# The first batch's queries, scores and masks put earlier, and a first mixer group that begins over two of three blocks of channels

## The chip, the cores and the metric

One core of a Trainium2 chip runs the whole kernel. The metric is device time in microseconds (us), the median over several executions. The kernel before takes 480.65 us (480.13 to 480.83 in 3 executions). Engines are called PE (TensorE), PEld (its weight loads), ACT (ScalarE), DVE (VectorE), POOL (GpSimd) and SP (SyncE, which issues the DMAs). "L223" is line 223 of the kernel before.

## The reference

Two stages, over 4 batches of 768 positions and 8 heads of 48 channels (384 in all):

```python
# attention, per batch and head
f = 1 / (1 + exp(-f_logit))
for t in range(S):
    state = f[t][:, None] * state + outer(k[t], v[t])
    y[t] = q[t] @ state
# x: y with the heads side by side, (batch, 768, 384)
# mixer
h = (x.transpose(0, 2, 1) @ U @ V).transpose(0, 2, 1)   # U 768 x 32, V 32 x 768
u = x + h
out = u + relu(u @ w_ch1) @ w_ch2                       # 384 x 1536, 1536 x 384
```

The mixer's weights come as 8-byte floats and are turned into 4-byte ones on the chip.

## The kernel before, in words

**Attention.** A unit is one pair of heads of one batch, so there are 16, four in a batch (`HP` = 4). A unit's 768 positions are cut into 12 chunks of 64. For each chunk the kernel forms scores of queries against keys (`scores`, L843), masks them (`mask`, L856 on DVE), multiplies them with v (`inner`, L948), makes the chunk's contribution to the state (`states`, L891, copied to `added` by ACT in L898), and joins the contributions to running states with a scan on DVE (`scan`, L913), which are then read with the queries (`read`, L930). `kept` (L870, copy L874) turns the weighted keys. The front half of a unit prepares its operands: `gates` (transposes L680, sigmoid on ACT, L742 and L743 in later batches), `keep` (scan of the gates' logs L747 on DVE, then the copy L752 on ACT), `keys`, `read_back`, and `queries` (transposes L680, then DVE L692). `front(n, ...)` and `rear(n, ...)` hand out these pieces of unit n by name. The results are copied into `x` (L954).

**Mixer.** The low rank part is L223 (`low_rank_of`), L232 (`added_up_of`) and L248 (`mix_of`), ending in additions to `x` on DVE (L197). Then pairs of position blocks (groups `a` = 0, 1, 2) are turned by `turn(a)` (six transposes L261 and one ACT copy L262) and multiplied: `ch1(a, j)` is 12 products L273 of 128 x 256 and one relu L283 on ACT, over columns 2j and 2j + 1 of w_ch1 in pieces of 128; `ch2` is L298. `ps_mm`, the pool of PSUM banks for most of these, has two buffers.

**Weights.** U, two parts of V, 12 column slices of w1 and 12 row slices of w2 are brought in by `weight_loader`. Each has four parts: `start` (a DMA of 8-byte words, L82), `halves` (ACT L91, L92), `join` (DVE L98, L99, L100) and, at the end of `join`, POOL's L101, which writes the slice. A conversion of a slice means all of halves and join. `ahead_by(n, weights)` makes a list of calls, each of which starts the transfer n places further on and converts its own slice. The first six slices of w1 are loaded into spare z buffers (`held` makes them free), all later ones into four buffers `w_raw`.

**Order.** Inside `manual_schedule` the order on PE, DVE and ACT is that of the code, written by hand; SP's loads are in the code's order as well up to `written.close()`. The first batch's four units run one after another with their pieces interleaved by hand; its mixer's first part follows, and then a loop in which the mixer's `ch1` pieces of the first batch, one conversion of a slice each, and (from piece `EARLY` on) pieces of the second batch's units alternate. What is left of the conversions is done after the loop. Two small fillers, `warm(2)` and `warm(3)` (L217), are products whose results nobody reads, each of 128 x 128 in a bank already in use; `busy` is the same on a bank of its own.

Of the kernel before, what the change touches and what calls it, by code (L numbers as in the profile page):

```python
# [10 lines left out]
F32 = mybir.dt.float32  # L11
# [100 lines left out]
def ahead_by(n, loads):  # L112


    def call(i):
        if i + n < len(loads):
            loads[i + n][0]()
        loads[i][1]()

    return [lambda i=i: call(i) for i in range(len(loads))]  # L120
# [36 lines left out]
class Mixer:  # L157
# [6 lines left out]
    def __init__(self, tc, b, x, U, V, w1, w2, sums, ident, blocks, out, two, three, zp, ps_big, ps_mm, wide=False,  # L164
                 z_all=None, room=None, pair=0):
        nc = tc.nc
        P = nc.NUM_PARTITIONS
        NCH, DM = x.shape[1], x.shape[2]
        R, FF = U.shape[2], w1.shape[2]
        NG = P // R  # L170
        NDC, NFC = DM // P, FF // P
# [39 lines left out]

        hs, last = {}, {}

        def warm(n):

            for _ in range(n):
                nc.tensor.matmul(last["pm"][:, DM : DM + P], lhsT=ident, rhs=ident, start=True, stop=True)  # L217

        def low_rank_of(cols):
            pm = last["pm"] = ps_mm.tile([P, 512], F32, name="ph", tag="mm")  # L220
            for c in range(NCH):
                g = slice((c % NG) * R, (c % NG + 1) * R)
                nc.tensor.matmul(pm[g, cols], lhsT=U[:, c, :], rhs=x[:, c, cols],  # L223
                                 start=(c < NG), stop=(c >= NCH - NG))
            if not hs:
                for i in range(2):
                    hs[i] = two.tile([P, DM], F32, name="h", bufs=2)
            nc.scalar.copy(hs[0][:, cols], pm[:, cols])

        def added_up_of(cols):  # L230
            pm = last["pm"] = ps_mm.tile([P, 512], F32, name="ph", tag="mm")
            nc.tensor.matmul(pm[:, cols], lhsT=blocks, rhs=hs[0][:, cols], start=True, stop=True)  # L232
            nc.scalar.copy(hs[1][:, cols], pm[:, cols])

# [15 lines left out]
                xv = bass.AP(a.tensor, a.offset, [list(a.ap[0]), [DM, 2], [NG * DM, m], [1, n]])  # L250
                add(xv, xv, pm, ALU.add)

        self.some = low_rank_of, added_up_of, mix_of, warm

        def turn(a):

# [10 lines left out]
        def ch1(a, j):  # L267

            pm = ps_mm.tile([P, 512], F32, name="pz", tag="mm")
            for i in range(2):  # L270
                for m in range(NDC):
                    o = (2 * j + i) * P
                    nc.tensor.matmul(pm[:, i * 2 * P : (i + 1) * 2 * P], lhsT=w1[:, m, o : o + P],  # L273
                                     rhs=uT[a][:, m, :], start=(m == 0), stop=(m == NDC - 1))
            c, k = divmod(2 * j, NI)
            if k == 0:

                if z_all is not None and not (wide and c == 1):
                    i = a if wide else (2 * a + c) % 3
                    z[a, c] = z_all[:, i * NI : (i + 1) * NI, :]  # L280
                else:
                    z[a, c] = zp.tile([P, NI, 2 * P], F32, name="zw" if wide and c == 1 else "z")
            nc.scalar.activation(z[a, c][:, k : k + 2, :].rearrange("p i t -> p (i t)"), pm, AF.Relu)  # L283

        def store(t, o):
            nc.sync.dma_start(out=out[b, t * P : (t + 1) * P, :], in_=o)
# [201 lines left out]
def factored_path(ctx, tc, q, k, v, f_logit, moe_U, moe_V, moe_w_ch1, moe_w_ch2, out, ok):  # L488
# [475 lines left out]
    def front(n, *names):  # L964

        if n >= NU:
            return []
        if n not in ahead:
            ahead[n] = dict(zip(("gates", "keep", "keys", "read_back", "queries"), prepare(n)))
        return [ahead[n].pop(nm) for nm in names]  # L970

    def rear(n, *names):

        if not 0 <= n < NU:
            return []
        if n not in here:
            here[n] = dict(zip(("kept", "states", "scan", "scores", "read", "inner", "mask", "spread"), attend(n)))
        return [here[n].pop(nm) for nm in names if nm in here[n]]
# [53 lines left out]
    with tc.manual_schedule(engines={nc.vector.engine, nc.scalar.engine}):  # L1032


        idle = ps_mm.tile([P, 512], F32, name="idle", tag="mm")

        def busy(n, cols=DM):
            for _ in range(n):
                nc.tensor.matmul(idle[:, 0:cols], lhsT=blank[:, 0:P], rhs=blank[:, 0:cols], start=True, stop=True)

        written = ExitStack()
        written.enter_context(tc.manual_schedule(engines={nc.sync.engine}))
        busy(3)
        for piece in front(0, "gates", "read_back", "keep"):
            piece()
        load(1, "k", "q")
        load(2, "f")
        load(1, "v")
        loads = ahead_by(early + FIRST, weights)
        halves, join = [[w[i] for w in weights[:early]] for i in (2, 3)]  # L1050
        done, rest = slice(0, 2 * (HP - 1) * D), slice(2 * (HP - 1) * D, DM)

        def held():
            for i in range(2, FIRST, 2):
                t = zp.tile([P, NFC // 2, 2 * P], F32, name="zw").rearrange("p i t -> p (i t)")
                nc.scalar.copy(t[:, 0:1], x_tiles[0][:, 0, 0:1])
                spare.extend([t.bitcast(U64)[:, 0:WP], t.bitcast(U64)[:, WP : 2 * WP]])
            for load_w in weights[early + 2 : early + FIRST]:
                load_w[0]()
            load(HP, "f", "k", "q", "v")  # L1060

        for n in range(HP):
            last = n + 1 == HP
            pieces = rear(n - 1, "scan", "mask") + front(n, "keys")
            if last:
                pieces += join[:1]
            if n == 0:
                pieces += front(n, "queries") + rear(n, "spread", "kept") + [lambda: busy(1, 2 * P)]
                pieces += front(n + 1, "gates") + rear(n, "scores", "states") + front(n + 1, "read_back", "keep")
                for piece in pieces:  # L1070
                    piece()
                load(2, "k", "q")
                load(3, "f")
                load(2, "v")
                continue
            pieces += rear(n, "spread") + rear(n - 1, "read") + rear(n, "kept")
            if last:
                pieces += halves[1:2] + front(n, "queries") + rear(n - 1, "inner") + [held] + join[1:2] + rear(n, "states")
                pieces += halves[2:] + rear(n, "scores")
            else:  # L1080
                pieces += rear(n - 1, "inner") + front(n + 1, "gates") + front(n, "queries") + rear(n, "states", "scores")
                pieces += (halves[:1] if n + 2 == HP else []) + front(n + 1, "read_back", "keep")
            for piece in pieces:
                piece()
            if n == 1:
                weights[0][0]()
                load(3, "k", "q")
                for load_w in weights[1:early]:
                    load_w[0]()
                load(3, "v")  # L1090
                for load_w in weights[early : early + 2]:
                    load_w[0]()
        m = mixer(0)
        low_rank_of, added_up_of, mix_of, warm = m.some
        for piece in rear(n, "scan", "mask") + join[2:]:
            piece()
        for load_w in weights[early + FIRST : early + FIRST + early]:
            load_w[0]()
        load(HP + 1, "f", "k", "q", "v")
        written.close()  # L1100
        low_rank_of(done)
        warm(2)
        loads[early]()
        for piece in rear(n, "read"):
            piece()
        added_up_of(done)
        for piece in rear(n, "inner"):
            piece()
        mix_of(done, range(0, NBL - 2, 2))
        low_rank_of(rest)  # L1110
        mix_of(done, range(NBL - 2, NBL, 2))
        added_up_of(rest)
        mix_of(rest)
        warm(3)
        loads[early + 1]()
        for t in [starts] + fz:
            nc.vector.memset(t, 0.0)
        loads = loads[early + 2 :]

        start = m.before[3:5] + m.firsts[0:1] + m.before[5:]  # L1120

        EARLY = 6
        second = chain(front(HP, "gates", "keep", "keys", "read_back", "queries"), steps(HP, 2 * HP + 1))
        for i, (_, piece) in enumerate(start + m.firsts[1:]):
            piece()
            if loads:
                loads.pop(0)()
            if i >= EARLY:
                next(second)()
        for f in loads:  # L1130
            f()
        n = len(m.seconds) // (NBL // 2)
        todo, after = m.seconds[:-n], m.seconds[-n:]

        attention(second, 12 + 10 * HP - (len(start) + len(m.firsts) - 1 - EARLY), todo)
        m = start_mixer(1, after)
        for f in to_sum:
            f()
# [380 lines left out]
```

## Time and profile before

| | before |
|---|---|
| median of 3 executions | 480.65 us |
| profiled execution | 480.69 us |
| its span | 479.0 us |
| mean granted TensorE clock | 0.999 |
| PE busy | 462.1 us (96%) |
| PEld busy | 399.0 us (83%) |
| DVE busy | 346.0 us (72%) |
| ACT busy | 181.0 us (38%) |
| POOL busy | 36.1 us (8%) |

The span is the time between the first and the last record of the core; 1.7 us of the execution lie around it. Busy shares are averages over the whole span. A row of the timeline gives the start and the duration in us, the engine, the line, the operation and its tiles, and in brackets the idle time of that engine before it with the work that ended it. PE rows of many products are drawn together ("x48").

### The profile page before, as it was taken

Reading aid. Unit: us, or ns where it says so; the run is one execution under the profiler, and the core shown is the slowest. Engines: PE = TensorE matmul, PEld = TensorE weight load, DVE = VectorE, ACT = ScalarE, POOL = GpSimd, SP = SyncE. Lnnn points to the kernel's source line nnn. Section 1 sums busy time; section 2 is a strip of 40 time slices with the busy share of each in tenths; the row PEclk is TensorE's granted clock in tenths of the full one; section 3 lists DMA queues with packets and bytes.
Section 4 is the critical chain, followed back from the end, with each engine's and each line's share of the span. In section 5 each row is a group of like instructions: output and inputs, shape, how many; then the busy total and the mean of one; then the engine's idle time right before and its main releaser. Section 6 shows DMA issues by size and latency. Waiting matters only on the chain.

```text
span 479.0 us, 12800 instructions
## 1 busy us (share of the span) xinstructions
PE 462.1 (96%) x5557; PEld 399.0 (83%) x5557; DVE 346.0 (72%) x557; ACT 181.0 (38%) x338; POOL 36.1 (8%) x48
## 2 busy tenths in 40 slices
PE   7989999999999899999999999999999999999995
PEld 5876888876665478798899888899979999999995
DVE  4557978798999575767766547997796886858642
ACT  5675766664444123434341423542311311212200
POOL 2001445442000000000000000000000000000000
PEclk9999999999999999999999999999999999999999
DMA  9988996667787422253425200100000000000001
GB/s 145 151 160 219 210 235 156 161 117 103 115 120 117 84 41 26 26 77 78 64 38 100 41 33 3 27 3 21 16 1 1 35 1 18 18 0 34 1 34 40
DMA packets 158680, 34.36 MB, mean 72 GB/s; under 512 B 149206, under 2 KB 157078, under 8 KB 158614
## 3 DMA queue, kind: packets, MB, share of 16 engines
q1 hardware_dynamic: 158614, 33.44, 38.2%
q8 instruction: 46, 0.75, 0.7%
q14 instruction: 20, 0.16, 0.1%
HBM read 28.70 MB, written 4.72 MB: 70 GB/s over the span
## 4 chain that ended last, share of the span: by engine, by line
PE 75%; DVE 11%; ACT 5%; issue 3%; DMA 3%; SPq 1%; POOL 0%; DVEq 0%; ACTq 0%
PE pw L327 26%; PE pz L273 20%; PE pp L425 12%; PE sc L843 2%; PE y L948 2%; PE y L930 2%; DVE late L765 2%; PE po L298 2%; DVE late L747 1%; DVE added L913 1%; PE put L261 1%; PE pt L870 1%; PE ds L891 1%; PE pt L710 1%; PE pu L207 1%
## 5 line engine op out<-in xcount | busy, mean ns | idle before, releaser
L273 PE MATMUL pz<-uT,w 128*128 128x256 f32 x504 | 114.7, 382 | 1.8 <-ACT z_all L283 1.3
L273 PEld LDWEIGHTS pz<-uT,w 128*128 128x128 f32 x504 | 93.7, 190 | 15.8 <-ACT z_all L283 2.1
L327 PE MATMUL pw<-w,z_all 128*128 128x192 f32 x216 | 37.7, 329 | 0.0
L327 PE MATMUL pw<-zw,w_raw 128*128 128x192 f32 x216 | 37.3, 327 | 0.0
L327 PEld LDWEIGHTS pw<-zw,w_raw 128*128 128x128 f32 x216 | 35.2, 190 | 0.7 <-DVE w_raw L197 0.6
L327 PEld LDWEIGHTS pw<-w,z_all 128*128 128x128 f32 x216 | 35.0, 190 | 0.7
L101 POOL TENSOR_TENSOR w<-w_y,w_r 128x384 int32<-128x384 int32 x24 | 31.5, 1313 | 40.0 <-DVE w_y L100 34.4
L283 ACT ACTIVATE z_all<-pz 128x512 f32<-128x512 f32 x33 | 19.7, 597 | 33.0 <-PE pz L273 32.9
L425 PE MATMUL pp<-v_nat,late 128*128 128x128 f32 x224 | 28.8, 275 | 0.0
L425 PEld LDWEIGHTS pp<-v_nat,late 128*128 128x128 f32 x224 | 27.0, 192 | 0.0
L418 ACT ACTIVATE other<-other 128x512 f32<-128x512 f32 x18 | 11.3, 633 | 39.9 <-DVE other L197 39.9
L918 ACT COPY st<-added 128x576 f32<-128x576 f32 x12 | 14.7, 1225 | 30.5 <-DVE added L913 30.5
L298 PE MATMUL po<-w,z_all 128*128 128x384 f32 x72 | 24.9, 493 | 1.2 <-DVE o L197 1.2
L298 PE MATMUL po<-w,zw 128*128 128x384 f32 x72 | 25.3, 496 | 0.0
L747 DVE TENSOR_TENSOR_SCAN late<-fz,late 128x768 f32<-128x768 f32 x12 | 21.1, 1756 | 4.0 <-ACT fz L742 3.6
L856 DVE TENSOR_TENSOR A<-sc,causal 128x768 f32<-128x768 f32 x16 | 15.1, 947 | 10.8 <-PE sc L843 10.8
L298 PEld LDWEIGHTS po<-w,z_all 128*128 128x128 f32 x72 | 13.3, 190 | 10.0 <-DVE o L197 1.8
L298 PEld LDWEIGHTS po<-w,zw 128*128 128x128 f32 x72 | 13.1, 190 | 9.7 <-issue 1.2
L765 DVE TENSOR_TENSOR_SCAN late<-fz,other 128x768 f32<-128x768 f32 x12 | 21.0, 1747 | 0.2
L418 ACT ACTIVATE z_all<-z_all 128x512 f32<-128x512 f32 x12 | 7.6, 632 | 32.8 <-DVE z_all L197 32.8
L898 ACT COPY added<-ds 48x576 f32<-48x576 f32 (+1 forms) x28 | 17.8, 636 | 3.5 <-PE ds L891 3.2
L327 PE MATMUL pw<-w,other 128*128 128x192 f32 x108 | 18.6, 327 | 0.0
(216 smaller groups left out, 840.1 us busy)
## 6 DMA issues: line engine op xcount, KB each, us to landing
w_raw<-in_moe_w_ch_dram SPq DMA_DIRECT2D x18, 384.0 KB, 3.6
out_dram<-o SPq DMA_DIRECT2D x24, 192.0 KB, 1.9
v_nat<-in_v_dram SPq DMA_DIRECT2D x16, 144.0 KB, 2.7
v_nat<-in_v_dram SPq DMA_DIRECT2D x32, 72.0 KB, 3.4
zw<-in_moe_w_ch_dram SPq DMA_DIRECT2D x6, 384.0 KB, 5.2
late<-in_f_logit_dram SPq DMA_DIRECT2D x10, 96.0 KB, 2.8
late<-in_k_dram SPq DMA_DIRECT2D x10, 96.0 KB, 2.9
late<-in_q_dram SPq DMA_DIRECT2D x10, 96.0 KB, 2.6
```

The lines of the kernel that those rows point to most:

```text
L101: nc.gpsimd.tensor_tensor(dst.bitcast(I32), shaped(y.bitcast(I32)), shaped(r), ALU.add)
L273: nc.tensor.matmul(pm[:, i * 2 * P : (i + 1) * 2 * P], lhsT=w1[:, m, o : o + P], rhs=uT[a][:, m, :], start=(m == 0), stop=(m == NDC - 1))
L283: nc.scalar.activation(z[a, c][:, k : k + 2, :].rearrange("p i t -> p (i t)"), pm, AF.Relu)
L298: nc.tensor.matmul(pm, lhsT=z[a, i // NI][:, i % NI, s * P : (s + 1) * P], rhs=w2[:, i, :], start=(i == 0), stop=(i == NFC - 1))
L327: nc.tensor.matmul(pm[:, n * HM : (n + 1) * HM], lhsT=lhs[:, i, :], rhs=rhs[:, i, :], start=(i == 0), stop=(i == NI - 1))
L418: nc.scalar.activation(dst, dst, AF.Relu, scale=float(SIGNS[n]))
L425: nc.tensor.matmul(pm[:, i, r * P : (r + 1) * P], lhsT=room["w"](wn)[:, r * P : (r + 1) * P], rhs=x_node(a, xn), start=((xn, wn) == of[0]) ...
L747: nc.vector.tensor_tensor_scan(backwards(X, S - 1, S), backwards(f, S, S), backwards(ends, S - 1, S), 0.0, ALU.mult, ALU.add,)
L765: nc.vector.tensor_tensor_scan(Y, f[:, 0:S], starts, 0.0, ALU.mult, ALU.add)
L856: nc.vector.tensor_tensor(T["A"], sc[:, :, 0 : NBL * C].rearrange("p h (c i) -> p h c i", i=C), causal.unsqueeze(1).unsqueeze(1).broadcast ...
L898: nc.scalar.copy(added[r, 1:].rearrange("p (e c s) -> p e c s", c=NBL, s=2), ds[r, :, 0 : NBL * D].rearrange("p s (c e) -> p e c s", e=D),)
L918: nc.scalar.copy(st, states.rearrange(by_e, c=NCH))
```

## The change

It puts work of the first batch and its mixer in another order. There are five parts.

- *Units 0 to 3:* `queries` and `scores` come ahead of `states`, and the mask L856 directly after the scores, so ahead of the scan L913. In unit 3 the scan follows its states at once.
- *Fillers:* `warm` is removed. `busy(2, 256)` stands where `warm(2)` was, nothing where `warm(3)` was.
- *First mixer group:* `turn_of` turns some of the three 128-channel blocks of a group, `ch1_of` multiplies some of the pairs (column i, block m) of a `ch1` into one bank, and `ch1_end` is the relu. The first group turns and multiplies blocks 0 and 1, then `turn(1)` is done, and block 2 comes last.
- *Weights:* four transfers into `w_raw` are begun up front rather than three, and `ahead_by` reaches one place further. The conversion of w1[1] goes to a place after the read of unit 3, ahead of the mixer's additions L197; that of w1[2] stands behind the first ch1, and the memsets L1117 behind it.
- *Loop:* the first six pieces are followed by 2, 1, 2, 1, 1, 0 conversions, all later ones by one. `EARLY` goes from 6 to 3, as the loop has three fewer pieces at its start, so the second batch's pieces meet the same `ch1` pieces. Two conversions are left after the loop, w2[10] and w2[11]; before, one.

```diff
-        def warm(n):
-
-            for _ in range(n):
-                nc.tensor.matmul(last["pm"][:, DM : DM + P], lhsT=ident, rhs=ident, start=True, stop=True)
-
...
+        def turn_of(a, ms):
+
+            if a not in uT:
+                uT[a] = three.tile([P, NDC, 2 * P], F32, name="uT")
+                last["put"] = ps_big.tile([P, 2, 512], F32, name="put", tag="big")
+            pt = last["put"]
+            for m in ms:
+                for s in range(2):
+                    nc.tensor.transpose(pt[:, s, m * P : (m + 1) * P], x[:, 2 * a + s, m * P : (m + 1) * P], ident)
+            g = slice(ms[0], ms[-1] + 1)
+            nc.scalar.copy(
+                uT[a][:, g].rearrange("p m (s t) -> p s m t", s=2),
+                pt[:, :, ms[0] * P : (ms[-1] + 1) * P].rearrange("p s (m t) -> p s m t", t=P),
+            )
+
+        def ch1_of(a, j, *products):
+
+            if "pz" not in last:
+                last["pz"] = ps_mm.tile([P, 512], F32, name="pz", tag="mm"), []
+            pm, had = last["pz"]
+            for i, m in products:
+                o = (2 * j + i) * P
+                nc.tensor.matmul(pm[:, i * 2 * P : (i + 1) * 2 * P], lhsT=w1[:, m, o : o + P], rhs=uT[a][:, m, :],
+                                 start=not had, stop=(m == NDC - 1), skip_group_check=True)
+                had.append((i, m))
+            if len(had) == 2 * NDC:
+                ch1_end(a, j, pm)
+                del last["pz"]
...
-        loads = ahead_by(early + FIRST, weights)
+        loads = ahead_by(early + FIRST + 1, weights)
...
-            pieces = rear(n - 1, "scan", "mask") + front(n, "keys")
-            if last:
-                pieces += join[:1]
+            pieces = rear(n - 1, "scan") + (join[:1] if last else []) + front(n, "keys") + rear(n, "spread")
+            pieces += rear(n - 1, "read") + front(n, "queries") + rear(n, "kept")
             if n == 0:
-                pieces += front(n, "queries") + rear(n, "spread", "kept") + [lambda: busy(1, 2 * P)]
-                pieces += front(n + 1, "gates") + rear(n, "scores", "states") + front(n + 1, "read_back", "keep")
...
+                pieces += [lambda: busy(1, 2 * P)] + front(1, "gates") + rear(0, "scores", "mask", "states")
+            elif last:
+                pieces += halves[1:2] + join[1:2] + rear(n - 1, "inner") + [held] + rear(n, "scores", "mask")
+                pieces += halves[2:] + rear(n, "states", "scan") + join[2:]
+            else:
+                pieces += rear(n - 1, "inner") + front(n + 1, "gates") + rear(n, "scores", "mask", "states")
+            if n + 2 == HP:
+                pieces += halves[:1]
+            if not last:
+                pieces += front(n + 1, "read_back", "keep")
...
-            pieces += rear(n, "spread") + rear(n - 1, "read") + rear(n, "kept")
-            if last:
-                pieces += halves[1:2] + front(n, "queries") + rear(n - 1, "inner") + [held] + join[1:2] + rear(n, "states")
-                pieces += halves[2:] + rear(n, "scores")
-            else:
-                pieces += rear(n - 1, "inner") + front(n + 1, "gates") + front(n, "queries") + rear(n, "states", "scores")
-                pieces += (halves[:1] if n + 2 == HP else []) + front(n + 1, "read_back", "keep")
...
-        for piece in rear(n, "scan", "mask") + join[2:]:
-            piece()
-        for load_w in weights[early + FIRST : early + FIRST + early]:
+        for load_w in weights[early + FIRST : early + FIRST + 4]:
             load_w[0]()
         load(HP + 1, "f", "k", "q", "v")
         written.close()
         low_rank_of(done)
-        warm(2)
+        busy(2, 2 * P)
         loads[early]()
         for piece in rear(n, "read"):
             piece()
+        loads[early + 1]()
         added_up_of(done)
...
         added_up_of(rest)
+        turn_of(0, range(2))
         mix_of(rest)
-        warm(3)
-        loads[early + 1]()
+        ch1_of(0, 0, (0, 0), (0, 1))
+        turn_of(0, range(2, NDC))
+        ch1_of(0, 0, (1, 0), (1, 1))
+        m.before[4][1]()
+        ch1_of(0, 0, (0, 2), (1, 2))
+        loads = loads[early + 2 :]
+        loads.pop(0)()
         for t in [starts] + fz:
             nc.vector.memset(t, 0.0)
-        loads = loads[early + 2 :]
-
-        start = m.before[3:5] + m.firsts[0:1] + m.before[5:]
-
-        EARLY = 6
+
+        start = m.before[5:]
+
+        EARLY = 3
         second = chain(front(HP, "gates", "keep", "keys", "read_back", "queries"), steps(HP, 2 * HP + 1))
         for i, (_, piece) in enumerate(start + m.firsts[1:]):
             piece()
-            if loads:
-                loads.pop(0)()
+            for f in loads[: (2, 1, 2, 1, 1, 0)[i] if i < 6 else 1]:
+                loads.remove(f)
+                f()
             if i >= EARLY:
                 next(second)()
         for f in loads:
             f()
```

`m.before[3:]` are `turn(0)`, `turn(1)` and `turn(2)`; `m.firsts` are the `ch1` pieces, for each j over the three groups.

More of the change, by code (lines that the diff above doesn't have):

```diff
@@ L212, in __init__ @@
         hs, last = {}, {}
-        def warm(n):
-            for _ in range(n):
-                nc.tensor.matmul(last["pm"][:, DM : DM + P], lhsT=ident, rhs=ident, start=True, stop=True)
         def low_rank_of(cols):
-            pm = last["pm"] = ps_mm.tile([P, 512], F32, name="ph", tag="mm")
+            pm = ps_mm.tile([P, 512], F32, name="ph", tag="mm")
             for c in range(NCH):
@@ L230, in added_up_of @@
         def added_up_of(cols):
-            pm = last["pm"] = ps_mm.tile([P, 512], F32, name="ph", tag="mm")
+            pm = ps_mm.tile([P, 512], F32, name="ph", tag="mm")
             nc.tensor.matmul(pm[:, cols], lhsT=blocks, rhs=hs[0][:, cols], start=True, stop=True)
@@ L251, in mix_of @@
                 add(xv, xv, pm, ALU.add)
-        self.some = low_rank_of, added_up_of, mix_of, warm
         def turn(a):
@@ L274, in ch1, with ch1_end @@
                                      rhs=uT[a][:, m, :], start=(m == 0), stop=(m == NDC - 1))
+            ch1_end(a, j, pm)
[22 more added lines that the diff above has]
+            if len(had) == 2 * NDC:
+                ch1_end(a, j, pm)
+                del last["pz"]
+        def ch1_end(a, j, pm):
             c, k = divmod(2 * j, NI)
@@ L283, in ch1 @@
             nc.scalar.activation(z[a, c][:, k : k + 2, :].rearrange("p i t -> p (i t)"), pm, AF.Relu)
+        self.some = low_rank_of, added_up_of, mix_of, turn_of, ch1_of
         def store(t, o):
@@ L1063, in factored_path @@
             last = n + 1 == HP
-            pieces = rear(n - 1, "scan", "mask") + front(n, "keys")
-            if last:
-                pieces += join[:1]
+            pieces = rear(n - 1, "scan") + (join[:1] if last else []) + front(n, "keys") + rear(n, "spread")
+            pieces += rear(n - 1, "read") + front(n, "queries") + rear(n, "kept")
             if n == 0:
-                pieces += front(n, "queries") + rear(n, "spread", "kept") + [lambda: busy(1, 2 * P)]
-                pieces += front(n + 1, "gates") + rear(n, "scores", "states") + front(n + 1, "read_back", "keep")
-                for piece in pieces:
-                    piece()
+                pieces += [lambda: busy(1, 2 * P)] + front(1, "gates") + rear(0, "scores", "mask", "states")
[8 more added lines that the diff above has]
+                pieces += front(n + 1, "read_back", "keep")
+            for piece in pieces:
+                piece()
+            if n == 0:
                 load(2, "k", "q")
@@ L1074, in factored_path @@
                 load(2, "v")
-                continue
-            pieces += rear(n, "spread") + rear(n - 1, "read") + rear(n, "kept")
-            if last:
-                pieces += halves[1:2] + front(n, "queries") + rear(n - 1, "inner") + [held] + join[1:2] + rear(n, "states")
-                pieces += halves[2:] + rear(n, "scores")
-            else:
-                pieces += rear(n - 1, "inner") + front(n + 1, "gates") + front(n, "queries") + rear(n, "states", "scores")
-                pieces += (halves[:1] if n + 2 == HP else []) + front(n + 1, "read_back", "keep")
-            for piece in pieces:
-                piece()
-            if n == 1:
+            elif n == 1:
                 weights[0][0]()
@@ L1093, in factored_path @@
         m = mixer(0)
-        low_rank_of, added_up_of, mix_of, warm = m.some
-        for piece in rear(n, "scan", "mask") + join[2:]:
-            piece()
-        for load_w in weights[early + FIRST : early + FIRST + early]:
+        low_rank_of, added_up_of, mix_of, turn_of, ch1_of = m.some
+        for load_w in weights[early + FIRST : early + FIRST + 4]:
             load_w[0]()
```

## The prediction

> **What bounds the kernel now.** I read the page first: TensorE (PE) is busy 462.1 us of 479.0, every slice at full clock, so this is a kernel in which a moved wait counts only where PE itself ends up waiting.
>
> ```profile
> span 479.0 us, 12800 instructions
> ...
> PE   7989999999999899999999999999999999999995
> ...
> DVE  4557978798999575767766547997796886858642
> ...
> PEclk9999999999999999999999999999999999999999
> ```
>
> The PE row has digits under 9 in the first fifth only, which is where the diff works; DVE is next to full there. A table by stage sharpens that: PE is busy 8.99 of 10 us in 10 to 20, 6.00 of 7 in 30 to 37, 8.42 of 9 in 37 to 46, 14.22 of 15 in 46 to 61, 11.77 of 12 in 61 to 73, 31.00 of 31 in 73 to 104, 12.99 of 13 in 104 to 117, and 352 of 362 after that. Almost no slack is left behind 61 us: a delay put there reaches the end, and a gain made before it survives only if nothing behind it holds PE. Next I read the timeline of 36 to 75 us. Columns: start, duration, engine, line, operation, out<-in, and in brackets the idle time and its releaser.
>
> ```profile
> 37.00 0.90 PE L891 MATMUL ds<-v_nat,kb 64*64 64x48 f32 x48
> ...
> 38.64 1.36 DVE L913 TENSOR_TENSOR_SCAN st<-added,whole 128x576 f32<-128x576 f32 x1 [0.52 <-ACT added L898]
> ...
> 40.21 0.71 PE L217 MATMUL ph<-ident 128*128 128x128 f32 x4 [0.50 <-ACT h L228]
> 40.85 1.24 PE L930 MATMUL y<-st,qT 48*64 48x48 f32 x44
> ...
> 46.92 0.94 PE L217 MATMUL ph<-ident 128*128 128x128 f32 x6
> ...
> 52.95 0.99 POOL L101 TENSOR_TENSOR w<-w_y,w_r 128x384 int32<-128x384 int32 x1 [2.61 <-ACT z_all L283]
> 53.12 1.05 DVE L99 TENSOR_SCALAR w_y<-w_y 128x384 uint32<-128x384 uint32 x1
> ...
> 66.09 0.55 ACT L91 ACTIVATE w_y<-w_raw 128x384 f32<-128x384 f32 x1 [0.61 <-DMA w_raw<-in_moe_w_ch_dram]
> ...
> 67.93 1.75 DVE L747 TENSOR_TENSOR_SCAN late<-fz,late 128x768 f32<-128x768 f32 x1
> ...
> 69.72 0.21 ACT L752 COPY least<-late 128x12 f32<-128x12 f32 x1 [2.62 <-DVE late L747]
> 69.84 0.59 ACT L283 ACTIVATE z_all<-pz 128x512 f32<-128x512 f32 x1
> ...
> 70.48 2.86 PE L273 MATMUL pz<-uT,w 128*128 128x256 f32 x12 [0.23 <-ACT z_all L283]
> ```
>
> See three things. The two L217 groups are filler, 0.71 and 0.94 us on PE. L99 takes 1.05 us beside POOL's L101. And a chain from conversion to PE: slice w1[9] waits for its transfer, then the scan L747 stands behind that conversion on DVE, the copy L752 behind the scan, the relu L283 behind the copy on ACT, PE behind the relu. Last, the timeline of 104 to 116.6 us:
>
> ```profile
> 109.88 0.36 DVE L98 TENSOR_SCALAR w_y<-w_y 128x384 f32<-128x384 f32 x1 [1.47 <-ACT w_y L91]
> ...
> 111.14 1.75 DVE L747 TENSOR_TENSOR_SCAN late<-fz,late 128x768 f32<-128x768 f32 x1
> 111.37 2.31 POOL L101 TENSOR_TENSOR w<-w_y,w_r 128x384 int32<-128x384 int32 x1 [2.70 <-DVE w_y L100]
> ...
> 113.10 1.28 ACT L898 COPY added<-ds 48x576 f32<-48x576 f32 x2
> 113.73 0.30 PEld L298 LDWEIGHTS po<-w,zw 128*128 128x128 f32 x2 [0.62 <-POOL w L101]
> ...
> 114.58 0.79 PEld L948 LDWEIGHTS y<-v_nat,A 64*64 64x64 f32 x48 [0.55 <-ACT added L898]
> ```
>
> Here the last conversion of all (w2[11]) already releases PE at 113.73, and the scan behind it, through L752 and L898, releases PE at 114.58: both without slack.
>
> **What the Trainium skill says.** "SBUF — State Buffer", section "Who interferes with whom": DVE's second port pair is GpSimd's, and the shared pair is an exclusive lock. The trace agrees: L99 takes 0.36 us with POOL idle (110.27) and 1.05 beside L101; L101 takes 1.00, but 2.31 beside a scan. "TensorE: Matmul & The Clock Gate", section "Architectural detail: the array is 16× 32×32, not 1× 128×128": ScalarE's and VectorE's queues are strictly first in, first out. The trace agrees: relu L283 starts at 69.84, just behind L752 at 69.72, though its product was done earlier. Same page, "What's actually happening": PE's clock falls after an idle window of about 3.4 us. No PE wait in the first mixer group reaches 1 us and the granted clock is 0.999, so the filler taken out should cost no clock.
>
> **The change part by part.** The profiled execution is 480.69 us: a span of 479.0 and 1.7 around it; the median shown is 480.65, so a sum against it also stands against the median.
>
> 1. *Units 0 to 2 (queries and scores earlier).* No instruction is added. SP issues its loads back to back there and waits for nothing until about 35.4 us (then 2.6 us on the ACT copy L1056); the order of these loads is unchanged, and landings pace the units (q of unit 2 lands at 23.8, k and q of unit 3 at 30.5 and 33.1). What hides the edit is that wait for data. Behind the moved L680 on PE stand kept and inner: if q is late they wait too, +0.3; if the freed PE time counts, −0.3. I take 0.
>
> 2. *Unit 3: scores and mask ahead, filler out.* v of unit 3 lands at 36.3 to 37.0 in both orders, so states (L891) stay at 37.0; scores (L843, 0.92) now lie before it instead of behind. L898, scan L913 still end at 40.0, but the mask (0.93 on DVE) is done before and the L217 filler (0.71, up to 40.92) is replaced by short products ahead of that. Read L930 starts at about 40.0, not 40.85: −0.85.
>
> 3. *First mixer group over two blocks.* The second filler, 0.94, goes; the same 12 transposes (1.47) and all products of ch1 stay, one more ACT copy appears (0.8 split in two). On DVE the conversion of w1[1] (0.35 + 0.36 + 0.56 = 1.27) now lies ahead of the three x adds L197, so these gain only 0.2 us, but what PE does next, mix and transposes of two blocks, no longer waits for all adds. Gain −0.85 − 0.94 = −1.8; bounds −1.6 and −1.8 at the gates' L680, which stood at 61.01. I take −1.7.
>
> 4. *Given back by the conversions.* w1[2] is now converted behind relu (0,0) on ACT, and behind it on DVE stand the memsets L1117 (0.70 + 1.51 = 2.21), then w1[3]. Products (0,0) can begin at 46.2; their 2.83 with the transposes among them (1.47 for all) end at 50.5, the relu at 51.1, L91 at 51.7, DVE's 1.27 at 53.0, the memsets at 55.2: w1[3] starts at 54.3 (were the products 0.9 sooner) to 55.2, where before it was 52.73. From there each slice takes 1.95 (L98 0.35, L99 1.05 beside POOL, L100 0.56): before 52.73, 54.67, 56.63, 58.58, 60.53, 62.48. Seven slices w1[3] to w1[9] are 13.65, so the scan L747 starts at 68.0 to 68.9; before, 67.93, since there w1[9] waited for its transfer to 65.78. That transfer is now issued one slot earlier (four loads up front on SP, ahead of unit 5's, which are late by one 384 KB load, 1.6 us, and needed some 20 us later: 0). Scan + 2.55 (1.75, 0.21, 0.59) releases PE's L273: 70.55 to 71.45 against 70.48. So the −1.7 is gone and X = +0.05 to +0.95; I take +0.4.
>
> 5. *Two conversions after the loop.* From the third stretch of the loop on each w2 slice is converted one piece later; 73 to 104 hides that (PE 31.00 of 31, w2 not needed). But w2[10] and w2[11] now both stand between the gates' activations L742, L743 and the scan L747. The first takes 109.88 to 111.14 as now, the second 1.95, as its L99 meets POOL. Scan at 113.1, L752 at 114.9, L898 to 116.3, L948 at 116.5 against 114.58; POOL's last L101 ends 115.6 against 113.68, so PE waits 2.0 more ahead of L298's last two. Behind PE stand L843 and everything after it. Y = +1.95, bounds 1.3 (no collision) and 2.1.
>
> Sum: X + Y = +0.4 + 1.95 = +2.35, so 480.69 + 2.35 = **483.0 us**; from the bounds 482.0 to 483.7.
>
> **The rivals.**
> - *The early gain stays (same).* If w1[9] is converted by 66.2 us, because the memsets slip beside ACT's part and w1[3] starts by 52.6, the relu isn't late: −1.7 + 1.95 = +0.25, 480.9. For it: DVE has 2.15 us idle at 64.5. Against: that idle time was spent waiting for a transfer, and before it the chain was full.
> - *No collision of POOL and DVE (faster).* With the changed neighbours L99 could come ahead of L101 instead of into it. A slice then takes 1.27, seven save 4.8 us, and X is the full −1.7. At 110 the second conversion costs 1.27, L101 is no longer stretched by the scan (2.31 to 1.00), and PE's waits of 0.62 and 0.55 go: Y = +0.1. Together −1.6, 479.1. It decides where L99's mean falls under about 0.8: there seven slices save 1.75, X = −1.35 and Y = about +1.3. For it: L99 is 0.36 at 110.27. Against: six slices in a row from 52.73 show 1.05.
> - *Conversion late for products (slower still).* PE reaches the products of w1[3] 1.7 earlier, at about 58.0 (the second half of 58.4 to 61.17, less 1.7), and by step 4 POOL ends that slice at 54.3 to 55.2 + 1.27 + 1.2, so 56.8 to 57.7. Were DVE or ACT 1.2 later there, w1[9] and the scan would be 1.2 late as well: 483.0 + 1.2 = 484.2.
> - *It does nothing early.* If landings pace unit 3's queries too, step 2's gain is nil; but step 4 takes the gain anyway, so X hardly moves: this is part of the main case.
>
> **How the numbers follow.** Main case 0.58 at 483.0; slower still 0.12 at 484.2; early gain stays 0.13 at 480.9; no collision 0.17 at 479.1. Within 0.2% of 480.65 means 479.7 to 481.6, about what a measurement of this kernel can tell from no change. Faster 0.17, same 0.13, slower 0.70. The range reaches from 479.4, which leaves out most of the last case, to 484.6, which holds the worse one; the main case alone is 482.0 to 483.7.
>
> **What would show it.** In the changed profile: L930 at about 40.0, no L217; the gates' L680 at about 59.3, not 61.01; w1[3]'s L98 at 54 to 55; scan L747 at 68.0 to 68.9 and a PE wait on L283 of 1.5 to 2 us about 71; then L98 twice before L747 at about 113.5, PE waiting some 2.5 us on POOL's L101, and L948 near 117. It is wrong if the relu's wait about 71 stays under 0.5 us, or if PE doesn't wait longer at L298's last two.

## The result, and the profile after

The changed kernel takes 483.48 us (482.86 to 485.15, 7 executions) against 480.65 (480.13 to 481.97, 7 executions); the ratio is 1.0065, 95% interval 1.0047 to 1.0083. It is slower by 2.8 us where 2.35 was forecast. Its profiled execution took 483.40 us, with a span of 481.7.

Lines have moved in the code: L680 is now L709, L747 is L776, L752 is L781, L283 is L310, L273 is L267 (L293 where `ch1_of` issues it), L298 is L327, L898 is L927, L913 is L942, L930 is L959, L948 is L977. The filler `busy` is L1068.

The page of the changed kernel, its span and three rows of the slices:

```profile
span 481.7 us, 12787 instructions
...
PE   7899979998999899999999999999999999999995
...
DVE  4567686798999755757766646997896886858642
...
PEclk9999999998999999999999999999999999999999
```

Two slices say where to look: the sixth of the PE row (60 to 72 us) has a 7 and the tenth (108 to 120 us) an 8, where the kernel before had 9s, and the tenth also shows a lower granted clock. The timeline of the changed kernel from 36 to 76 us (start, duration, engine, line, operation, out<-in, idle time and its releaser):

```profile
38.55 1.36 DVE L942 TENSOR_TENSOR_SCAN st<-added,whole 128x576 f32<-128x576 f32 x1 [1.18 <-ACT added L927]
...
38.86 1.13 PE L1068 MATMUL idle<-late 128*128 128x256 f32 x4
...
40.05 1.24 PE L959 MATMUL y<-st,qT 48*64 48x48 f32 x44
...
46.47 1.13 PE L293 MATMUL pz<-uT,w 128*128 128x256 f32 x4
...
55.00 0.30 DVE L98 TENSOR_SCALAR w_y<-w_y 128x384 f32<-128x384 f32 x1
...
56.59 1.05 DVE L99 TENSOR_SCALAR w_y<-w_y 128x384 uint32<-128x384 uint32 x1
...
58.88 0.82 PE L709 MATMUL pt<-ident,late 128*128 128x128 f32 x6
...
62.92 2.86 PE L267 MATMUL pz<-uT,w 128*128 128x256 f32 x12 [0.64 <-ACT z_all L310]
...
67.14 2.83 PE L267 MATMUL pz<-uT,w 128*128 128x256 f32 x12 [0.70 <-ACT z_all L310]
...
67.45 0.36 DVE L98 TENSOR_SCALAR w_y<-w_y 128x384 f32<-128x384 f32 x1 [1.42 <-ACT w_y L91]
...
68.72 1.75 DVE L776 TENSOR_TENSOR_SCAN late<-fz,late 128x768 f32<-128x768 f32 x1
...
70.50 0.21 ACT L781 COPY least<-late 128x12 f32<-128x12 f32 x1 [2.63 <-DVE late L776]
...
71.26 2.86 PE L267 MATMUL pz<-uT,w 128*128 128x256 f32 x12 [1.29 <-ACT z_all L310]
```

The read is 0.80 us earlier than before (40.05 against 40.85), the gates' L709 2.13 earlier (58.88 against 61.01). Twelve microseconds later nothing of it is left. PE has waited for relus three times (0.64, 0.70 and 1.29 us), the scan starts 0.79 later than before (68.72 against 67.93) and the products behind it 0.78 later (71.26 against 70.48). The first product of L327 is 0.77 late too (105.67 against 104.90), so what was lost by 71 us stays lost up to 105. Then the timeline from 104 to 120 us:

```profile
110.66 0.36 DVE L98 TENSOR_SCALAR w_y<-w_y 128x384 f32<-128x384 f32 x1 [1.47 <-ACT w_y L91]
...
111.92 0.35 DVE L98 TENSOR_SCALAR w_y<-w_y 128x384 f32<-128x384 f32 x1
...
112.31 1.05 DVE L99 TENSOR_SCALAR w_y<-w_y 128x384 uint32<-128x384 uint32 x1
...
113.86 1.75 DVE L776 TENSOR_TENSOR_SCAN late<-fz,late 128x768 f32<-128x768 f32 x1
114.09 2.31 POOL L101 TENSOR_TENSOR w<-w_y,w_r 128x384 int32<-128x384 int32 x1 [0.95 <-DVE w_y L100]
...
116.45 0.91 PE L327 MATMUL po<-w,zw 128*128 128x384 f32 x2 [1.95 <-POOL w L101]
...
117.29 1.36 PE L977 MATMUL y<-v_nat,A 64*64 64x48 f32 x48
```

Two conversions stand ahead of the scan, the second with its L99 at 1.05 beside POOL, and L977 starts at 117.29 instead of 114.58: 2.71 late, of which 1.94 arose here. 0.77 + 1.94 = 2.71 is the whole difference of the spans (2.7). The view of PE's waits from 45 to 125 us (in total, times, longest), first of the kernel before, then of the changed one, shows both losses:

```profile
PE pz L273 <- ACT uT L262: 0.5, 2, 0.3
...
PE pz L273 <- ACT z_all L283: 0.2, 1, 0.2
```

```profile
PE pz L267 <- ACT z_all L310: 2.6, 3, 1.3
PE po L327 <- POOL w L101: 2.0, 1, 2.0
```

The kernel before waits 1.5 us in this stretch in all, of which 0.2 are for a relu; the changed one waits 4.6 us, all for relus and POOL.

### The profile page after: what moved, and what is told of

Its sections match the earlier page's. It is cut to its first block, busy times and chain, and to the rows that moved or that the text cites. A ratio compares the mean times of both kernels' runs of the same rounds, so it can differ in the third digit from the quotient of the medians.

```text
span 481.7 us, 12787 instructions
## 1 busy us (share of the span) xinstructions
PE 462.5 (96%) x5551; PEld 399.2 (83%) x5551; DVE 345.8 (72%) x557; ACT 180.7 (38%) x339; POOL 36.1 (7%) x48
## 4 chain that ended last, share of the span: by engine, by line
PE 77%; DVE 11%; ACT 3%; issue 3%; SPq 2%; DMA 2%; POOL 1%; DVEq 0%; POOLq 0%; ACTq 0%
PE pw L356 26%; PE pz L267 18%; PE pp L454 12%; PE po L327 4%; PE y L959 3%; PE y L977 2%; PE sc L872 2%; PE ds L920 2%; PE pt L899 2%; PE pt L709 1%; PE put L255 1%; SPq L592 1%; DVE w_y L99 1%; DVE late L794 1%; PE pu L207 1%
## 5 line engine op out<-in xcount | busy, mean ns | idle before, releaser
L267 PE MATMUL pz<-uT,w 128*128 128x256 f32 x492 | 112.2, 383 | 3.8 <-ACT z_all L310 3.7
L267 PEld LDWEIGHTS pz<-uT,w 128*128 128x128 f32 x492 | 91.5, 190 | 17.9 <-ACT z_all L310 4.2
L101 POOL TENSOR_TENSOR w<-w_y,w_r 128x384 int32<-128x384 int32 x24 | 31.5, 1314 | 43.7 <-DVE w_y L100 43.7
L310 ACT ACTIVATE z_all<-pz 128x512 f32<-128x512 f32 x33 | 19.6, 597 | 33.1 <-PE pz L267 33.0
L327 PE MATMUL po<-w,zw 128*128 128x384 f32 x72 | 25.3, 496 | 2.0 <-POOL w L101 2.0
L327 PE MATMUL po<-w,z_all 128*128 128x384 f32 x72 | 25.0, 495 | 1.2 <-DVE o L197 1.2
L776 DVE TENSOR_TENSOR_SCAN late<-fz,late 128x768 f32<-128x768 f32 x12 | 21.1, 1755 | 4.0 <-ACT fz L771 3.6
L327 PEld LDWEIGHTS po<-w,zw 128*128 128x128 f32 x72 | 13.1, 190 | 11.6 <-POOL w L101 2.6
L327 PEld LDWEIGHTS po<-w,z_all 128*128 128x128 f32 x72 | 13.4, 192 | 10.1 <-DVE o L197 1.8
L98 DVE TENSOR_SCALAR w_y<-w_y 128x384 f32<-128x384 f32 (+3 forms) x27 | 11.1, 410 | 14.3 <-ACT w_y L91 14.2
L927 ACT COPY added<-ds 48x576 f32<-48x576 f32 (+1 forms) x28 | 17.8, 635 | 5.8 <-PE ds L920 5.7
```

Source lines behind the costliest of these rows:

```text
L101: nc.gpsimd.tensor_tensor(dst.bitcast(I32), shaped(y.bitcast(I32)), shaped(r), ALU.add)
L327: nc.tensor.matmul(pm, lhsT=z[a, i // NI][:, i % NI, s * P : (s + 1) * P], rhs=w2[:, i, :], start=(i == 0), stop=(i == NFC - 1))
L776: nc.vector.tensor_tensor_scan(backwards(X, S - 1, S), backwards(f, S, S), backwards(ends, S - 1, S), 0.0, ALU.mult, ALU.add,)
L927: nc.scalar.copy(added[r, 1:].rearrange("p (e c s) -> p e c s", c=NBL, s=2), ds[r, :, 0 : NBL * D].rearrange("p s (c e) -> p e c s", e=D),)
```

## The experiments

Theory: two waits make the difference, the relus behind a late chain of conversions at 60 to 71 us, and the second conversion behind the loop. Rivals: the second wait hides the first or is hidden by it; the fall of the clock has its own price; the early gain would have been lost in the kernel before as well. Unless said otherwise each edit is made to the changed kernel. All ratios are to the kernel before in the same batch of runs. The changed kernel was timed in the first batch only, and the median of the kernel before moved between batches (480.65, 480.57, 480.25 and 480.42 us). So what an edit is worth against the changed kernel is worked out from the two ratios, and is uncertain by about 1 us, as the changed kernel's own interval reaches 0.9 us to either side.

**The late conversion, taken out (e1) and put in alone (e3).**

```diff
-            for f in loads[: (2, 1, 2, 1, 1, 0)[i] if i < 6 else 1]:
+            for f in loads[: (2, 1, 2, 1, 1, 0)[i] if i < 6 else 2 if i == 9 else 1]:
```

> The changed kernel with one more conversion at the tenth piece of the loop, so that one (w2[11]) and not two is left after it. Theory (the second conversion behind the loop holds the scan L776 and POOL's last L101 by 1.95 us): about 483.5 - 1.9 = 481.6 us, PE's wait ahead of L327's last two back at about 0.6, L977 at about 115.4, and no fall of the clock behind it. Rival (what is lost is lost ahead of 73 us, and the wait at 114 to 116 only takes the place of a later one): 483.2 to 483.5. Rival (the fall of the clock at 118 us costs its own 1.1 us on top): about 480.5.

Measured: 482.30 us, ratio 1.0034 (1.0021 to 1.0048), by the ratios 1.5 us under the changed kernel where 1.9 was expected. The local step is as expected: from the first L327 to L977 it is 9.68 us (107.05 to 116.73), as in the kernel before (104.90 to 114.58), and 11.62 in the changed one. But the doubled tenth piece put the gates' scan behind a second conversion at 84 us. The scan starts 1.4 us later than in the changed kernel (87.67 against 86.29), and so does a relu behind it on ACT (96.89 against 95.51), for which PE then waits:

```profile
PE pz L267 <- ACT zw L310: 0.5, 1, 0.5
```

So the size of the wait is confirmed in place, and the edit gave some of it back elsewhere. The profiled execution was also late by 0.64 at L218 (38.41 against 37.77), which the edit doesn't reach: its granted clock stood at 0.50 from about 22.3 to 25.7 us.

In the kernel before:

```diff
-            if loads:
+            if loads and i != 12:
                 loads.pop(0)()
```

> The kernel before with no conversion at the 13th piece of its loop, so that each later one is a piece later and two are left after it: this part of the change alone. Theory: +1.95 us, about 482.6, PE's wait ahead of L298's last two at 2.5 us instead of 0.6. Rival (the loss comes only with the other parts): 480.7.

Measured: 482.18 us, ratio 1.0033 (1.0020 to 1.0047): +1.6 us, with a PE wait on POOL of 2.0 us ahead of L298's last two. This part of the change alone makes a kernel slower that has all the rest of the old order.

**The early chain (e2, e5, e6).** Memsets moved to DVE's idle stretch, ahead of the first products of `ch1(0,0)`:

```diff
         mix_of(rest)
+        for t in [starts] + fz:
+            nc.vector.memset(t, 0.0)
         ch1_of(0, 0, (0, 0), (0, 1))
...
         loads.pop(0)()
-        for t in [starts] + fz:
-            nc.vector.memset(t, 0.0)
```

> The changed kernel with the three memsets put behind the mixer's last addition L197, where DVE is idle for 4.15 us, instead of between the conversions of w1[2] and w1[3]. Theory (the memsets start the chain of conversions late, and that holds scan, relu and PE to 71 us): w1[3]'s L98 at about 52.8 and not 55.0, scan L776 at about 66.6, PE's waits on relus between 60 and 72 down from 2.6 to under 0.7, 481.5 us (-2.0). Rival (POOL or the relus behind conversions on ACT hold PE there whatever DVE does): 483.0 to 483.5, with the waits on L310 still above 2 us.

Measured: 482.43 us, ratio 1.0050 (1.0031 to 1.0068): by the ratios −0.7 us where −2.0 was expected, and not clear of noise. The timeline of this kernel shows why it gains so little:

```profile
52.96 1.00 POOL L101 TENSOR_TENSOR w<-w_y,w_r 128x384 int32<-128x384 int32 x1 [7.63 <-DVE w_y L100]
53.05 1.12 DVE L98 TENSOR_SCALAR w_y<-w_y 128x384 f32<-128x384 f32 x1 [0.24 <-ACT w_y L91]
```

w1[3] now meets w1[2]'s L101, from which the memsets had kept it apart: its L98 takes 1.12 us instead of 0.30. It begins 1.95 us earlier (53.05 against 55.00), but the next slice only 1.12 (55.08 against 56.20), and the scan 1.11 (67.61 against 68.72). The memsets cost the chain 1.1, not their 2.2. PE's waits on L310 are still 2.0 us in all, where the theory had under 0.7.

> The changed kernel with the fifth and sixth entries of the loop's counts exchanged, (2, 1, 2, 1, 0, 1): slice w1[9] is converted behind the gates' scan and not ahead of it. Theory (at 71 us PE waits for a relu that stands behind a copy, a scan and w1[9]): the scan L776 at about 66.7 rather than 68.72, PE's third wait on L310 (1.29 us at 71.26) gone, 482.2 us (-1.3). Rival (the time is lost in the POOL and relu waits from 57 to 67 us, and w1[9] moved makes the next relus late instead): 483.0 to 483.8.

```diff
-            for f in loads[: (2, 1, 2, 1, 1, 0)[i] if i < 6 else 1]:
+            for f in loads[: (2, 1, 2, 1, 0, 1)[i] if i < 6 else 1]:
```

Measured: 481.87 us, ratio 1.0038 (1.0027 to 1.0050): by the ratios −1.3 us, as the theory has it, for a swap of two counts. PE's waits on L310 fall from three, 2.6 us in all, to two, 1.4 us in all; the third one was that of the scan standing behind w1[9].

```diff
         ch1_of(0, 0, (0, 0), (0, 1))
+        loads = loads[early + 2 :]
+        loads.pop(0)()
         turn_of(0, range(2, NDC))
         ch1_of(0, 0, (1, 0), (1, 1))
         m.before[4][1]()
         ch1_of(0, 0, (0, 2), (1, 2))
-        loads = loads[early + 2 :]
-        loads.pop(0)()
```

> The changed kernel with the conversion of w1[2] moved up behind the first products of ch1(0,0), so that its ACT part lies ahead of the relu of that ch1 and its DVE part and the memsets fill DVE's idle 4.15 us. Theory (the chain of conversions begins late because w1[2] waits behind that relu, and holds PE by 2.6 us in three waits on L310): w1[3]'s L98 at about 51.3 instead of 55.0, all three waits together under 0.5 us, 481.0 us (-2.5). Rival (as with the memsets, POOL's collision takes half of it back): 482.2 us (-1.2). Rival (ACT's two activations delay the copy uT and with it PE): over 483.5.

Measured: 480.97 us, ratio 1.0017 (1.0002 to 1.0031): by the ratios −2.3 us, where the theory has −2.5. w1[3]'s L98 starts at 52.16, earlier than 55.00 but not at 51.3. The view of PE's waits in the same stretch:

```profile
PE po L327 <- POOL w L101: 1.9, 1, 1.9
PE pz L267 <- ACT z_all L310: 0.8, 1, 0.8
```

The wait on POOL is untouched; the early ones fall from 2.6 to 0.8 (not under 0.5).

**Both, and then no conversion left (e7, e8).** On top of the last edit:

```diff
-            for f in loads[: (2, 1, 2, 1, 1, 0)[i] if i < 6 else 1]:
+            for f in loads[: (2, 1, 2, 1, 1, 1)[i] if i < 6 else 1]:
```

> As the run before, and the loop's counts (2, 1, 2, 1, 1, 1), so that each later conversion is back at the kernel before's piece and one is left behind the loop. Theory (the two losses add, and are the whole of the difference): 1.9 under the run before, so about 479.1 us, 1.5 under the kernel before: the early gain of the change is then kept. Rival (the conversion added at about 71 us holds the second batch's scans there and PE waits again): 480.0 to 480.7.

Measured: 478.89 us, ratio 0.9972 (0.9963 to 0.9982): 2.1 under the run before. The two losses add, and without them the rest of the change is a gain over the kernel before.

```diff
-            for f in loads[: (2, 1, 2, 1, 1, 1)[i] if i < 6 else 1]:
+            for f in loads[: (2, 1, 2, 1, 1, 1)[i] if i < 6 else 2 if i == 8 else 1]:
```

> As the run before, and two conversions instead of one at the ninth piece of the loop (DVE is idle for 1.95 us at 80 us), so that none is left behind the loop. Theory: PE's waits at 113.7 on POOL and at 114.6 on L927, 0.6 and 0.5 in the kernel before, go: about 478.2 us. Rival (as with the doubled tenth piece, a relu in the 90s is late and takes 0.5 back, or L977 waits for its scan all the same): 478.8 to 479.3.

Measured: 477.96 us, ratio 0.9953 (0.9936 to 0.9970), the lowest median here; its interval overlaps that of the run before, so the gain of 0.9 us isn't clear of noise. In its timeline the last products and L977 follow each other with no wait on POOL or on L927:

```profile
109.86 4.14 PE L327 MATMUL po<-w,zw 128*128 128x384 f32 x12
...
113.93 0.91 PE L977 MATMUL y<-v_nat,A 64*64 64x48 f32 x48
```

The rival's late relu is there as well (a wait of 1.1 us on `zw` L310), so some of the gain is still given away. From the first L327 to L977 it is 9.41 us (104.52 to 113.93) against 9.68 in the run before (101.99 to 111.67). So the waits of 0.6 and 0.5 us, which in the kernel before are those of PE's weight loads (PEld), cost its products only 0.27 us.

**What the other parts are worth (e4, e9, e10, e11).** In the kernel before, the changed kernel's loop over the first four units replaces the old one, with:

```diff
-        for piece in rear(n, "scan", "mask") + join[2:]:
-            piece()
...
-        warm(2)
+        busy(2, 2 * P)
...
-        warm(3)
```

> The kernel before with the first batch's units in the changed order and the fillers as in the changed kernel, but its own mixer group, transfers, loop and conversions. Theory (before 61 us PE gains, but slice w1[9] lands at about 65.8 and holds scan and relu to 70.5): the gates' L680 at about 59.4 to 59.8 rather than 61.01, PE's wait at 70.5 longer by as much, and the time 480.4 us, at most 0.3 under the kernel before. Rival (the gain is kept, since only the changed kernel's conversions eat it): 479.0 to 479.3. Rival (without filler the clock falls): over 481.

Measured: 480.49 us, ratio 0.9992 (0.9976 to 1.0009): no difference, as expected, but the path expected isn't shown. L680 started at 61.02, not at 59.4 to 59.8. Four lines of the timeline:

```profile
37.75 0.87 PE L891 MATMUL ds<-v_nat,kb 64*64 64x48 f32 x48
...
40.86 1.23 PE L930 MATMUL y<-st,qT 48*64 48x48 f32 x44
...
47.72 1.31 PE L261 MATMUL put<-ident,x 128*128 128x128 f32 x10 [0.36 <-DVE x L197]
...
67.27 0.56 ACT L91 ACTIVATE w_y<-w_raw 128x384 f32<-128x384 f32 x1 [1.80 <-DMA w_raw<-in_moe_w_ch_dram]
```

The read came no earlier than before (40.86 and 40.85): in this execution the granted clock stood at 0.50 from about 21.8 to 25.2 us, and the states started at 37.75 instead of 37.00. So it says nothing on what the new order and `busy` are worth up to the read. From there on it is plain: without `warm(3)` the transposes wait for the last addition and go on at 47.72; with it they began at 47.69. From the read to L680 it is 20.16 us in both kernels. The filler lay in a wait that was there anyway. And w1[9] landed more than 1 us later than in the profile of before, so the run doesn't separate a gain lost at the transfer from one never made.

Starting from the fastest kernel: the old loop over the units, with `scan`, `mask` and the last `join` behind it.

```diff
+        for piece in rear(n, "scan", "mask") + join[2:]:
+            piece()
         for load_w in weights[early + FIRST : early + FIRST + 4]:
```

> The last kernel (early w1[2], none left, 477.96 us) with the order of the first batch's units as in the kernel before (scan and mask of unit 3 behind its scores). Theory (with the conversions out of the way the units' order is worth what the read L959 moves, 0.85 us): about 478.8, read at about 40.8. Rival (v of unit 3, or DVE's adds, pace what follows, and the order is worth nothing): 477.9 to 478.1.

Measured: 478.44 us, ratio 0.9967 (0.9955 to 0.9980), overlapping that of the fastest. Its read starts at 40.18, that of the fastest kernel at 40.34, so the order doesn't move the read as the theory had it. By the ratios it is 0.7 us slower, which is not clear of noise: the order of the units shows no worth here, but the times alone don't exclude one of about 1 us.

```diff
-        turn_of(0, range(2))
         mix_of(rest)
-        ch1_of(0, 0, (0, 0), (0, 1))
         loads = loads[early + 2 :]
         loads.pop(0)()
-        turn_of(0, range(2, NDC))
-        ch1_of(0, 0, (1, 0), (1, 1))
+        m.before[3][1]()
         m.before[4][1]()
-        ch1_of(0, 0, (0, 2), (1, 2))
+        m.firsts[0][1]()
```

> The last kernel (477.96 us) with the first mixer group as in the kernel before: turn(0), turn(1), then the whole of ch1(0,0), all behind mix_of(rest). Theory (transposes then wait for the last addition L197, so that products begin at about 48.6 instead of 46.5 and PE stands idle meanwhile): about 479.1 us. Rival (the change's early gain comes from the fillers taken out, 0.94 us of it, and the group's order is worth under 0.3): 478.0 to 478.3.

Measured: 480.54 us, ratio 1.0006 (0.9990 to 1.0021): by the ratios 2.5 us over the fastest, more than either theory had. In the profiled executions (479.59 and 477.96) the products begin at 48.42 instead of 46.75, the gates' L709 is 0.76 later (59.51 against 58.75), and a wait on L197 is back:

```profile
PE put L255 <- DVE x L197: 0.4, 1, 0.4
```

The read varies between executions (39.92 here, 40.34 in the other). Counted from it, L709 comes after 19.59 us instead of 18.41, so the group's order is worth 1.18 us there. That this order has worth is shown, as the two intervals of the ratio lie apart; where the rest of the 2.5 arises is not, as executions of both kernels spread over 3 us and more.

```diff
-        busy(2, 2 * P)
```

> The last kernel (477.96 us) without the two filler products busy(2, 256) ahead of unit 3's read. Theory (PE waits there for the scan, with or without filler): 477.9 to 478.1. Rival (the idle time that opens lowers the granted clock): more than 478.5, with the clock under 1 behind 39 us.

Measured: 478.25 us, ratio 0.9959 (0.9946 to 0.9972): no difference. PE waits 1.1 us ahead of the read instead, and the mean clock stays at 0.999 in the profiled execution.

Not taken out alone were the fourth transfer begun up front and the earlier conversion of w1[1].

## Why the prediction was right or wrong

The sign, the mechanism and, within the range, the size were right: 483.0 forecast, 483.48 measured. Both losses arose where they were forecast. Inside the steps some terms were wrong and made up for each other.

- *Step 1, units at nothing.* Not contradicted: e9 finds no worth in their order that is clear of noise.
- *Step 2, read at 40.0.* It came at 40.05, but the source was put too widely. The scan ends at 40.00 in the kernel before and at 39.91 in the changed one; the read starts 0.85 us behind it in the one and 0.14 in the other. The difference is the filler: L217 wrote into the bank that ACT copies from, so it began only behind that copy, at 40.21, and ended at 40.92; `busy` has a bank of its own and ran from 38.86 to 39.99, beside the scan. In e3, with the old filler, the read comes 0.88 us behind the scan; in e7 and e8, with `busy`, 0.15 and 0.14. The read itself varies between executions of one order by more than the 0.85 forecast (39.12 in e7, 40.34 in e8), so that the forecast time was met so closely is in part luck.
- *Step 3, −1.7 at the gates' transposes.* Measured −2.13: −0.80 at the read and −1.33 behind it, where step 3 had −0.85. The terms were wrong. The second filler's 0.94 was counted as gain, and e4 shows that in the old group it is worth nothing, since the transposes wait for L197 without it. The order of the group, which was named but got no number of its own, is worth 1.18 by e10. No run has the new group with the old filler.
- *Step 4, X = +0.4 (0.05 to 0.95).* Measured +0.78. w1[3] at 55.00 and the scan at 68.72 lie within the times given, at the late end. The collision that spaces the slices by 1.95 us (the exclusive lock of "SBUF — State Buffer", section "Who interferes with whom", in the Trainium skill) goes on: L99 takes 1.05 us in five of the seven slices. But the sum of seven slices came out (13.72 us for 13.65) because two errors cancel. The first and the last slice meet no POOL and take 1.20 and 1.27 us, which saves 1.4; and DVE stands idle for 1.42 us ahead of w1[9], whose L91 on ACT starts only at 66.86, behind the gates' activations and a relu. e5 and e6 show that the conversions, and not the products, hold PE: by the ratios they take back 1.3 and 2.3 us without a change in PE's work. One wait of 1.5 to 2 us was forecast at 71; there were three, of 0.64, 0.70 and 1.29, from 62 us on.
- *Step 5, Y = +1.95.* Measured 1.94 between L327 and L977, and 1.6 in the time of e3.
- *The rivals.* No collision: refuted, though not by much, as L99's mean over the seven slices is 0.85 us, where the line was drawn at 0.8. The early gain stays: refuted by the wait at 71.26. Conversion late for products: it happened in part. PE's weight load for w1[3] waited 0.54 us for POOL at 57.4, and the 36 products of that stretch took 8.35 us, against 7.94 in e2 and e6, where w1[3] is earlier. These 0.4 us didn't decide the time, as the scan behind w1[9] released PE only at 71 us.
- *Clock.* The prediction saw no danger in the fillers taken out, and e11 agrees. But its reason, that no wait reaches 1 us, is no safe one: the last section has falls of the clock after waits of 1 us and less, and one at the new wait at 114 us, which was not foreseen. The statement that behind 61 us "a delay put there reaches the end" held for the 2.71 us, but not for the 1.4 us that this fall cost at first.

## What to carry to other kernels

A gain ahead of a chain that is already full on another engine is worth only what that chain lets through: before moving PE's work earlier, find the next place where PE waits for that engine, and price the chain up to there, with the collisions that its steps will meet and with what the third engine in it, here ACT, has to do first. A step postponed by one place in a loop comes out at the loop's end, where it may stand ahead of a scan that everything waits for; count what is left over there. Here a filler cost nothing while its engine would have waited anyway, unless it wrote where another engine still read.

## What the runs showed of the hardware

The clock fell after waits shorter than the prediction thought to matter. The windows view of PE in the changed kernel (stretch, length, busy and count, granted clock, DMA share, GB/s):

```profile
114.00:116.00 2.00, 0.50 (x2) 1.00 0.94 128
116.00:117.00 1.00, 0.55 (x2) 1.00 0.69 73
117.00:118.00 1.00, 1.00 (x35) 0.78 0.06 16
118.00:119.00 1.00, 1.00 (x49) 0.50 0.27 43
...
120.00:121.00 1.00, 1.00 (x13) 0.52 0.97 128
121.00:122.00 1.00, 1.00 (x4) 1.00 0.38 35
```

After a wait of 1.95 us PE ran at half its clock for about 3.4 us (117.6 to 121.0). The Trainium skill ("TensorE: Matmul & The Clock Gate", section "What's actually happening") names an idle window of about 3.4 us, free-running; here PE was idle for less. It doesn't happen each time: with the same wait of nearly 2 us, the clock fell in the profiled executions of the changed kernel and of the one with early memsets (e2), and did not in those of e3, e5 and e6. It fell after shorter waits as well: in e1 after two of 0.77 and 0.87 us, in e4 after two of 0.54 and 1.00 us, each pair within 3 us, while one wait of 1.36 us at the same place in the changed kernel was followed by no fall. Each of the four falls lasted about 3.4 us. What decides between fall and no fall isn't shown.

The price of the fall in the changed kernel was absorbed. PE was 4.08 us behind the kernel before at 120.73, but 2.69 at 158.55: waits that the kernel before has in between (0.47, 0.25 and 0.40 us) were taken up. And executions of the changed kernel with a mean clock of 0.999 took 483.46, 483.48 and 483.74 us, no less than the profiled one with 0.994.
